# Attention, two feed-forward layers on one core: the first silu placed behind a root, other banks seeded, and copies of Strassen products put first in their step

## Chip, core and metric

The kernel runs on one core of a Trainium2 chip. The metric is the device time of one execution in microseconds (us), median of several runs. It has four compute engines that matter here: TensorE (PE, matmuls), VectorE (DVE), ScalarE (ACT) and GpSimd (POOL); SyncE (SP) issues most DMAs.

## What is computed

Causal attention over 2 x 12 heads (448 positions, 64 wide), then a feed-forward layer with a hard-swish-like gate, then a second one with RMS norm and silu(gate) * value. Cut to the parts that matter:

```python
x = attention(q, k, v)                      # 896 tokens x 768
h = x @ w_in                                # 768 -> 2048
x = (h * clip(h + 3, 0, 6) / 6) @ w_out     # 2048 -> 768
xn = x / sqrt(mean(x * x) + 1e-6) * rms_g   # the root, per token
g = xn @ w_gate                             # 768 -> 1536
val = xn @ w_val
return (g / (1 + exp(-g)) * val) @ w_out2   # 1536 -> 768
```

The weights arrive as float64 and are turned into float32 on the chip. Every product is made of three passes (`mm3`, L205 to L214): each operand is split into a high part and a low part (names that end in hi and lo), and hi*hi, hi*lo and lo*hi are added in one PSUM bank.

## The kernel before

The 896 tokens stand in two groups of 448 (g = 0 and 1), and a matmul is 128 x 128 by 448 columns. Work is recorded in steps: a loop (L974 to L985) runs, in each step, first what is due (`begin_step`), then takes matmuls from the generator `products`, nine to a step once attention is over (`AFTER`). `at(delay, fn)` puts a function at the end of the list of a later step, `soon(fn)` puts it at the front of the next step's list. So the steps set the order of the instructions on each engine, and nothing else does: an engine takes them in that order, and waits where an operand isn't there.

`ff1_out` makes the second layer's input y, and `ff1_y`, `rms_sum` and `rms_root` make the RMS factor of a group. For a group: a matmul with ones (n, L604) sums the squares over partitions, ACT takes the root (L608), DVE the reciprocal (L609), DVE scales the six tiles of y (L621), and `y_split` and `y_low` split them (ACT L627, DVE L634). For group 1 this falls into the time in which PE already works on group 0 of `ff2_plain`.

`ff2_plain` makes the first two (`PLAIN`) column tiles of gate and value for both groups, by plain products: eight products of 18 matmuls, in PSUM banks f0_0 to f0_3 (group 0: gate, value, gate, value) and f1_0 to f1_3 (group 1). `ff2_gate` takes the silu of a gate bank (ACT L695), `ff2_val` multiplies it by the value bank (DVE L700). Two value banks are then kept in the list `spare`:

```python
            if n == 0:
                at(1, ff2_gate, g, m, ps)
            else:
                at(2, ff2_val, g, m, ps)
                if m == PLAIN - 1:
                    spare.append(ps)
```

Here m is 1 for f0_3 and f1_3, so these two are kept.

`ff2_strassen` makes the other ten column tiles m = 2 to 11, both groups at once, as seven products a tile (Strassen-Winograd, q = 1 to 7; below "product (q,m)"), nine matmuls each. For m = 2 and 3 they are interleaved in the order (1,2) (1,3) (2,2) (2,3) (7,2) (6,2) (7,3) (5,2) (6,3) (4,2) (5,3) (3,2) (4,3); from there on a tile is (1,m) (3,m-1) (7,m) (6,m) (2,m) (5,m) (4,m). The products accumulate in three banks: (1,m) and (2,m) in fx_m, (7,m) and (4,m) in fr_m, and (6,m), (5,m), (3,m) in a bank y taken from `spare`, which starts from a copy of (1,m). After each product `ff2_combine` (L856) does one thing: after q = 1 ACT copies fx into y (L861); after 7 ACT copies fr to c22 (L864); after 6 ACT copies y to c21 (L867); after 2 ACT takes the silu of fx (L870); after 5 and 4 DVE adds to c22 and c21 (L873, L876); after 3 DVE multiplies (L882) and gives the bank back to `spare`. So (2,m) must wait until the copy of (1,m) has read fx, and (5,m) until the copy to c21 has read y.

Beside this, weights of the next tiles are made ready by `pair_begin`'s schedule: ACT narrows float64 (L160, L164), DVE joins (L169), subtracts (L777, L798), and both split (ACT L766, L783; DVE L771, L788). The last stage, `strassen`, multiplies by w_out2.

Of the kernel before, what the change touches and what calls it, by code (L numbers as in the profile page):

```python
# [33 lines left out]
PLAIN = 2  # L34
# [17 lines left out]
def fused_kernel(ctx: ExitStack, tc, qa, qb, ka, kb, v, w_in, w_out, w_gate, w_val, w_out2, rms_g, out):  # L52
# [13 lines left out]
    def psum(name):  # L66
        return pspool.tile([128, 512], F32, tag="ps", name=name)
# [21 lines left out]
    def at(delay, fn, *args):  # L89
        due[clock["now"] + delay].append((fn, args))  # L90

    def soon(fn, *args):
        due[clock["now"] + 1].insert(0, (fn, args))
# [103 lines left out]
    def w_tile(n, j):  # L197

        if n not in used and not IN2 <= n < OUT2:
            used.add(n)  # L200
            splits.pop(n - 2, None)
            at(1, w_split)
        return tuple(t[:, j * 128:(j + 1) * 128] for t in splits[n])

    def mm3(ps, w, x, first, last, again=False):  # L205

        whi, wlo = w
        xhi, xlo = x
        nc.tensor.matmul(ps, whi, xhi, start=first, stop=False, skip_group_check=again)  # L209
        yield  # L210
        nc.tensor.matmul(ps, whi, xlo, start=False, stop=False, skip_group_check=again)  # L211
        yield
        nc.tensor.matmul(ps, wlo, xhi, start=False, stop=last, skip_group_check=again)  # L213
        yield  # L214
# [446 lines left out]
    def ff2_plain(w0):  # L661

        for t, (g, i) in enumerate((g, i) for g in range(2) for i in range(4)):
            m, n = divmod(i, 2)
            if t == 0:
                splits.pop(w0 - 2, None)
                splits.pop(w0 - 1)
                at(1, pair_high, PLAIN, 0)
                at(2, pair_low, PLAIN, 0)
                at(4, pair_load, PLAIN + 1, 0)  # L670
                at(5, pair_load, PLAIN + 1, 1)
            elif t == 4:
                pair_begin(PLAIN + 1)
            elif t in (5, 6, 7):
                splits.pop(w0 + t - 5)
            if t == 6:
                at(1, pair_high, PLAIN, 1)
                at(2, pair_low, PLAIN, 1)
            ps = psum(f"f{g}_{i}")[:, :NT]
            for k in range(NK):  # L680
                q = ((1, 2), (0, 4))[g][k // KH]
                yield from mm3(ps, w_tile(w0 + i, k), ops[q, k % KH], k == 0, k == NK - 1)
            if n == 0:
                at(1, ff2_gate, g, m, ps)
            else:
                at(2, ff2_val, g, m, ps)
                if m == PLAIN - 1:
                    spare.append(ps)
        splits.pop(w0 + 3)
        for j in range(KH):  # L690
            ops.pop((0, j))
# [42 lines left out]
    def pair_begin(m):  # L734
        at(1, pair_narrow, m, 0)
        at(2, pair_narrow, m, 1)
        at(3, pair_high, m, 0)
        at(4, pair_low, m, 0)
        at(4, pair_first, m)
        at(5, pair_second, m)  # L740
        at(6, pair_third, m)
        at(7, pair_high, m, 1)
        at(8, pair_low, m, 1)
        if m + 1 < NF2:
            at(4, pair_load, m + 1, 0)
            at(5, pair_load, m + 1, 1)
# [65 lines left out]
    def pair_tile(q, m, j):  # L812
        if q in (5, 6, 7):
            key, o = (m, "t", q), 0
        else:
            key, o = {1: ((m, 0), 0), 2: ((m, 0), 384), 4: ((m, 1), 0), 3: ((m, 1), 384)}[q]
        w = tuple(t[:, o + j * 128:o + j * 128 + 128] for t in ph[key])
        if j == KH - 1 and q not in (1, 4):
            ph.pop(key)
        return w  # L820
# [3 lines left out]
    def ff2_strassen():  # L824
        a, b = PLAIN, PLAIN + 1
        order = [(1, a), (1, b), (2, a), (2, b), (7, a), (6, a), (7, b), (5, a), (6, b), (4, a), (5, b), (3, a), (4, b)]
        for m in range(b + 1, NF2):
            order += [(1, m), (3, m - 1)] + [(q, m) for q in (7, 6, 2, 5, 4)]
        order.append((3, NF2 - 1))
        for q, m in order:  # L830
            if (q, m) == (6, a) or q == 1 and b < m < NF2 - 1:
                pair_begin(m + 2 if m == a else m + 1)
            if q == 1 and m + 1 == NF2:
                state["limit"] = len(srcs)
                for n in range(NC_BUF):
                    at(1 + n, w_load)
                for n in range(NW - 1):
                    at(4 + n + 3 * (n // 3), w_split)
                for p in range(NF2 // 2):
                    at(1 + p // 2, a_fetch, ORDER[0], p)  # L840
                    at(4 + p // 2, a_split, ORDER[0], p)
                for p in range(3):
                    at(5 + p, a_fetch, ORDER[1], p)
            name = {1: "x", 2: "x", 7: "r", 4: "r"}.get(q, "y")
            if q in (1, 7):
                fb[name, m] = psum(f"f{name}_{m}")[:, :NT]
            ps = fb[name, m]
            for j in range(KH):
                yield from mm3(ps, pair_tile(q, m, j), ops[q, j], q in (1, 7) and j == 0, j == KH - 1,
                               q not in (1, 7))  # L850
                if m == NF2 - 1:
                    ops.pop((q, j))
            at(1, ff2_combine, q, m)
        spare.clear()

    def ff2_combine(q, m):  # L856
# [56 lines left out]
    def products():  # L913
        yield from ff1_in(0, 0)
        plan_preps(0, *PREPS[0])
        yield from ff1_in(1, NP1)
        yield from ff1_out(0, 2 * NP1)
        at(1, w_split)
        plan_preps(PREPS[0][2], *PREPS[1])
        pair_early(PLAIN)  # L920
        yield from ff1_out(1, 3 * NP1)
        yield from ff2_plain(IN2)
        yield from ff2_strassen()
        yield from strassen(OUT2)
# [117 lines left out]
```

## Time and profile before

| | |
|---|---|
| median of 3 runs | 576.29 us (575.6 to 584.03) |
| the profiled execution | 577.63 us |
| its span, first to last instruction | 575.8 us |
| busy: PE, DVE, ACT, POOL | 563.0, 411.0, 392.3, 85.3 us |
| granted TensorE clock, mean of the span | 0.994 |

All times of instructions are from the one profiled execution and count from its first instruction. Rows of the timeline give start, duration, engine, source line, operation, output<-inputs, and, in square brackets, how long the engine sat idle just before and what ended that idle time. Names are without buffer numbers: f is any of the banks f0_0 to f1_3, yhi and ylo any split tile of y. Matmuls overlap, so the distance between two starts says more than the duration of one.

### The profile page before, as it was taken

Reading aid. Unit: us, or ns where it says so; the run is one execution under the profiler, and the core shown is the slowest. Engines: PE = TensorE matmul, PEld = TensorE weight load, DVE = VectorE, ACT = ScalarE, POOL = GpSimd, SP = SyncE. Lnnn points to the kernel's source line nnn. Section 1 sums busy time; section 2 is a strip of 40 time slices with the busy share of each in tenths; the row PEclk is TensorE's granted clock in tenths of the full one; section 3 lists DMA queues with packets and bytes.
Section 4 is the critical chain, followed back from the end, with each engine's and each line's share of the span. In section 5 each row is a group of like instructions: output and inputs, shape, how many; then the busy total and the mean of one; then the engine's idle time right before and its main releaser. Section 6 shows DMA issues by size and latency. Waiting matters only on the chain.

```text
span 575.8 us, 9080 instructions
## 1 busy us (share of the span) xinstructions
PE 563.0 (98%) x3048; PEld 491.7 (85%) x3048; DVE 411.0 (71%) x796; ACT 392.3 (68%) x768; POOL 85.3 (15%) x130
## 2 busy tenths in 40 slices
PE   8899999999999999999999999899999999999997
PEld 6567777777899999999999998789999999999996
DVE  4676676767468857555598769969797877866861
ACT  6997878787567768876686778475766565654430
POOL 4665636262100000001001100000000000000000
PEclk9989999999999999999999999999999999999999
DMA  7949776754357888996799913027744517576841
GB/s 217 295 142 280 223 244 204 247 177 142 106 201 254 314 318 295 335 319 225 274 334 387 364 59 141 24 103 271 249 156 181 201 48 258 183 261 205 278 145 64
DMA packets 51231, 125.59 MB, mean 218 GB/s; under 512 B 6768, under 2 KB 30256, under 8 KB 51184
## 3 DMA queue, kind: packets, MB, share of 16 engines
q1 hardware_dynamic: 50752, 124.66, 63.2%
q8 instruction: 24, 0.39, 0.3%
q10 hardware_dynamic: 432, 0.34, 0.2%
q14 instruction: 23, 0.19, 0.1%
HBM read 93.36 MB, written 31.62 MB: 217 GB/s over the span
## 4 chain that ended last, share of the span: by engine, by line
PE 79%; ACT 8%; DVE 7%; DMA 3%; issue 2%; SPq 0%; POOL 0%; ACTq 0%; DVEq 0%
PE h L213 7%; PE h L209 7%; PE h L211 7%; PE y L209 5%; PE y L213 5%; PE y L211 5%; PE o L396 4%; PE t L370 4%; PE s L319 4%; PE f L211 3%; PE f L213 3%; PE f L209 3%; ACT sm L336 3%; PE fr L213 2%; PE fr L211 2%; PE fr L209 2%
## 5 line engine op out<-in xcount | busy, mean ns | idle before, releaser
L185 ACT CAST whi<-c 128x768 fp32r<-128x768 f32 x89 | 74.1, 835 | 40.2 <-DVE c L169 18.0
L191 DVE TENSOR_TENSOR wlo<-c,whi 128x768 fp32r<-128x768 f32 x89 | 88.2, 994 | 18.3 <-ACT whi L185 16.7
L213 PE MATMUL h<-xh,wlo 128*128 128x448 f32 x192 | 72.0, 375 | 0.0
L211 PE MATMUL h<-xl,whi 128*128 128x448 f32 x192 | 70.9, 369 | 0.0
L209 PE MATMUL y<-ghi,whi 128*128 128x448 f32 x192 | 70.5, 367 | 0.0
L209 PE MATMUL h<-xh,whi 128*128 128x448 f32 x192 | 70.4, 367 | 0.0
L213 PE MATMUL y<-ghi,wlo 128*128 128x448 f32 x192 | 70.0, 365 | 0.0
L211 PE MATMUL y<-glo,whi 128*128 128x448 f32 x192 | 69.3, 361 | 0.0
L354 POOL TENSOR_SCALAR sm<-sm,st 112x112 f32<-112x112 f32 (+1 forms) x96 | 55.7, 598 | 69.1 <-ACT pt L380 30.7
L336 ACT ACTIVATE sm<-sm,st 112x112 f32<-112x112 f32 (+3 forms) x96 | 49.5, 522 | 4.2 <-DVE st L329 4.2
L169 DVE SCALAR_TENSOR_TENSOR c<-c,raw 128x768 uint32<-128x768 uint32 x36 | 36.6, 1015 | 18.3 <-ACT raw L164 12.5
L213 PEld LDWEIGHTS h<-xh,wlo 128*128 128x128 f32 x192 | 36.0, 188 | 9.3 <-issue 6.7
L329 DVE CUSTOM_DVE_ANT_0 sm<-s,mask 112x112 f32<-112x112 f32 (+3 forms) x96 | 37.2, 443 | 9.2 <-PE s L319 9.0
L433 DVE SCALAR_TENSOR_TENSOR t<-t,h 128x448 f32<-128x448 f32 x32 | 19.7, 617 | 27.1 <-ACT t L429 27.0
L213 PEld LDWEIGHTS y<-ghi,wlo 128*128 128x128 f32 x192 | 35.9, 187 | 3.7 <-issue 0.2
L211 PEld LDWEIGHTS h<-xl,whi 128*128 128x128 f32 x192 | 36.0, 188 | 2.7
L211 PEld LDWEIGHTS y<-glo,whi 128*128 128x128 f32 x192 | 36.0, 188 | 2.7
L209 PEld LDWEIGHTS h<-xh,whi 128*128 128x128 f32 x192 | 36.2, 188 | 2.5
L209 PEld LDWEIGHTS y<-ghi,whi 128*128 128x128 f32 x192 | 36.0, 188 | 2.5 <-issue 0.2
L429 ACT ACTIVATE t<-h,half 128x448 f32<-128x448 f32 x32 | 20.3, 635 | 25.4 <-PE h L213 25.4
L370 PE MATMUL t<-ident,sm 112*112 112x112 f32 x240 | 33.6, 272 | 2.8 <-POOL sm L354 2.4
L600 POOL TENSOR_TENSOR sq<-sq,sq 128x448 f32<-128x448 f32 x8 | 9.9, 1238 | 171.4 <-ACT sq L589 164.0
(174 smaller groups left out, 1353.1 us busy)
## 6 DMA issues: line engine op xcount, KB each, us to landing
raw<-in_w_in SPq DMA_DIRECT2D x16, 768.0 KB, 5.4
raw<-in_w_out SPq DMA_DIRECT2D x16, 768.0 KB, 6.6
braw<-in_w_out SPq DMA_DIRECT2D x12, 768.0 KB, 6.3
c<-kept SPq DMA_DIRECT2D x21, 384.0 KB, 3.2
a<-left SPq DMA_DIRECT2D x35, 224.0 KB, 3.6
praw<-in_w_gate SPq DMA_DIRECT2D x10, 768.0 KB, 4.5
praw<-in_w_val SPq DMA_DIRECT2D x10, 768.0 KB, 6.4
keptin<-c SPq DMA_DIRECT2D x16, 384.0 KB, 2.7
```

The lines of the kernel that those rows point to most:

```text
L169: nc.vector.scalar_tensor_tensor(bits, bits, 3, z, ALU.logical_shift_left, ALU.bitwise_or)
L185: nc.scalar.copy(hi, c)
L191: nc.vector.tensor_sub(lo, c, f32(hi))
L209: nc.tensor.matmul(ps, whi, xhi, start=first, stop=False, skip_group_check=again)
L211: nc.tensor.matmul(ps, whi, xlo, start=False, stop=False, skip_group_check=again)
L213: nc.tensor.matmul(ps, wlo, xhi, start=False, stop=last, skip_group_check=again)
L319: nc.tensor.matmul(ps[:C, o:o + n], tq[64 * j:64 * j + 64, i * C:(i + 1) * C], tk[64 * j:64 * j + 64, 0:n], start=True, stop=True)
L329: nc.vector.tensor_tensor_reduce(dst, src, mask[:, S - n:], scale=-0.125, scalar=3e38, op0=ALU.add, op1=ALU.min, accum_out=st[u][:, 0, c:c ...
L336: nc.scalar.activation(dst, dst, AF.Exp, scale=-1.0, bias=st[u][:, 0, c:c + 1], accum_out=st[u][:, 1, c:c + 1])
L354: nc.gpsimd.tensor_scalar(t[:, o:o + n], t[:, o:o + n], c, 1.0, op0=ALU.mult, op1=ALU.mult)
L370: nc.tensor.transpose(banks[-1][:C, o:o + C], t[:, o0 + kc * C:o0 + (kc + 1) * C], ident[:C, :C])
L396: nc.tensor.matmul(ps[64 * j:64 * j + 64, HS - n:HS], tv[:, kc, 64 * j:64 * j + 64], t[:, o:o + n], start=kc == 0, stop=kc == nk - 1)
```

## The change

Three places. The silu of the very first gate bank is put three steps after its product instead of one. The two banks kept for the Strassen products are the value banks of group 0 (f0_1, f0_3) instead of the second value bank of each group (f0_3, f1_3). And `ff2_combine` is put at the front of the next step's list instead of its end.

```diff
             if n == 0:
-                at(1, ff2_gate, g, m, ps)
+                at(1 if t else 3, ff2_gate, g, m, ps)
             else:
                 at(2, ff2_val, g, m, ps)
-                if m == PLAIN - 1:
+                if g == 0:
                     spare.append(ps)
...
-            at(1, ff2_combine, q, m)
+            soon(ff2_combine, q, m)
```

On ACT, where group 1's root is taken (sq1_0 gets the root, n1 is the bank of summed squares, t0_0 and t0_1 are the silu of gate banks f0_0 and f0_2; - is before, + is now):

```order
 L766 CAST phi2_0_3942<-pe2_0_384_3750 128x384
+L608 ACTIVATE sq1_0_3414<-n1_3968,eps_73 128x448
 L695 ACT_TABLE_LOAD
-L695 ACTIVATE t0_0_3970<-f0_0_3925 128x448
-L608 ACT_TABLE_LOAD
-L608 ACTIVATE sq1_0_3414<-n1_3968,eps_73 128x448
+L695 ACTIVATE t0_0_3995<-f0_0_3925 128x448
 L627 CAST yhi0_0_4011<-y1_0_3412 128x448
 L627 CAST yhi0_1_4014<-y1_1_3513 128x448
 L627 CAST yhi0_2_4029<-y1_2_3652 128x448
 L627 CAST yhi4_0_4032<-y1_3_3744 128x448
-L695 ACT_TABLE_LOAD
```

The root now stands ahead of the first silu, and of the three table loads here one is left, between the root and the silu.

On ACT, at the first two Strassen products (fx_2 and fx_3 hold (1,2) and (1,3)):

```order
-L861 COPY f0_3_4018<-fx_2_4235 128x448
-L861 COPY f1_3_4207<-fx_3_4245 128x448
+L861 COPY f0_1_3959<-fx_2_4235 128x448
+L861 COPY f0_3_4018<-fx_3_4245 128x448
 L870 ACTIVATE s0_2_4275<-fx_2_4235 128x448
```

The two copies stand where they stood, but write other banks: the second one wrote f1_3, and now writes f0_3.

On ACT, a few products later, after (7,2) and (6,2) (c22_2 is the copy after (7,2), c21_2 the one after (6,2); pc4_0 and pc4_1 are the gate and value weights of tile 4):

```order
-L627 CAST yhi3_0_4301<-y0_3_3169 128x448
-L864 COPY c22_2_4304<-fr_2_4278 128x448
+L864 COPY c22_2_4301<-fr_2_4278 128x448
+L627 CAST yhi3_0_4303<-y0_3_3169 128x448
 L160 ACTIVATE pc4_0_4306<-praw4_0_4130 128x768
 L164 ACTIVATE praw4_0_4130<-praw4_0_4130 128x768
-L160 ACTIVATE pc4_1_4320<-praw4_1_4163 128x768
+L867 COPY c21_2_4319<-f0_1_3959 128x448
+L160 ACTIVATE pc4_1_4322<-praw4_1_4163 128x768
 L164 ACTIVATE praw4_1_4163<-praw4_1_4163 128x768
-L867 COPY c21_2_4325<-f0_3_4018 128x448
```

The copy to c22_2 moved ahead of one cast, and the copy to c21_2 ahead of the two narrowing instructions of the value weights.

## Rows read from the trace of the kernel before

**Rows 1.** The page, part 1: busy us (share of the span), instructions, by engine.

```profile
PE 563.0 (98%) x3048; PEld 491.7 (85%) x3048; DVE 411.0 (71%) x796; ACT 392.3 (68%) x768; POOL 85.3 (15%) x130
```

**Rows 2.** PE's waits in the whole span: line, releaser, us, times, longest.

```profile
PE fx L209 <- ACT f L861: 2.6, 1, 2.6
...
PE f L211 <- DVE ylo L634: 1.0, 1, 1.0
...
PE f L209 <- ACT c L867: 0.6, 1, 0.6
```

**Rows 3.** PE's timeline at its three waits and at the matmul n.

```profile
338.66 0.91 PE L604 MATMUL n<-sq,ones 128*128 128x448 f32 x2
...
339.62 0.37 PE L209 MATMUL f<-yhi,whi 128*128 128x448 f32 x1
...
348.71 0.37 PE L209 MATMUL f<-yhi,whi 128*128 128x448 f32 x1
350.09 0.48 PE L211 MATMUL f<-ylo,whi 128*128 128x448 f32 x1 [1.01 <-DVE ylo L634]
...
369.83 0.36 PE L213 MATMUL fx<-yhi,plo 128*128 128x448 f32 x1
372.80 0.47 PE L209 MATMUL fx<-yhi,phi 128*128 128x448 f32 x1 [2.61 <-ACT f L861]
...
379.99 0.37 PE L213 MATMUL fr<-yhi,ptlo 128*128 128x448 f32 x1
380.96 0.47 PE L209 MATMUL f<-yhi,pthi 128*128 128x448 f32 x1 [0.60 <-ACT c L867]
```

**Rows 4.** Stretches: length, busy us (instructions) by engine, granted clock, DMA share, GB/s.

```profile
333.40:364.57 31.17, 30.16 (x147) 27.29 (x146) 26.42 (x41) 24.54 (x40) 0.00 (x0) 1.00 0.20 72
364.57:392.00 27.43, 24.22 (x119) 21.80 (x117) 21.62 (x39) 16.57 (x28) 0.00 (x0) 1.00 0.22 83
392.00:495.79 103.79, 103.79 (x514) 96.26 (x513) 84.73 (x138) 65.01 (x111) 0.00 (x0) 1.00 0.56 197
345.67:373.20 27.53, 23.91 (x117) 21.50 (x116) 27.39 (x49) 18.58 (x33) 0.00 (x0) 1.00 0.21 77
```

**Rows 5.** ACT's timeline around group 1's root.

```profile
338.87 1.28 ACT L695 ACT_TABLE_LOAD   x1
340.16 0.55 ACT L695 ACTIVATE t<-f 128x448 f32<-128x448 f32 x1
340.72 1.28 ACT L608 ACT_TABLE_LOAD   x1
342.02 0.63 ACT L608 ACTIVATE sq<-n,eps 128x448 f32<-128x448 f32 x1
...
348.52 1.28 ACT L695 ACT_TABLE_LOAD   x1
```

**Rows 6.** DVE's timeline: reciprocal, first low parts, the multiplication of f1_3.

```profile
342.69 2.95 DVE L609 RECIPROCAL sq<-sq 128x448 f32<-128x448 f32 x1 [2.32 <-ACT sq L608]
...
349.42 3.30 DVE L634 TENSOR_TENSOR ylo<-y,yhi 128x448 fp32r<-128x448 f32 x6
...
371.53 0.61 DVE L700 TENSOR_TENSOR t<-f,t 128x448 f32<-128x448 f32 x1
```

**Rows 7.** ACT's timeline at the second copy of (1,m) and at c21_2.

```profile
372.23 0.52 ACT L861 COPY f<-fx 128x448 f32<-128x448 f32 x1 [5.12 <-DVE t L700]
...
376.80 0.53 ACT L864 COPY c<-fr 128x448 f32<-128x448 f32 x1 [0.82 <-PE fr L213]
377.23 0.90 ACT L160 ACTIVATE pc<-praw 128x768 f32<-128x768 f32 x1
...
380.40 0.51 ACT L867 COPY c<-f 128x448 f32<-128x448 f32 x1
...
381.55 0.57 ACT L627 CAST yhi<-y 128x448 fp32r<-128x448 f32 x1
```

**Rows 8.** ACT's waits in the whole span: line, releaser, us, times, longest.

```profile
ACT c L864 <- PE fr L213: 19.3, 9, 2.4
```

## Prediction

> **What bounds the kernel now.** I read the page first: PE is busy 98% of the span [rows 1], so time is won only where PE stands still, or by giving it less to do, and the change takes no matmul away. Next I read the list of what PE waits for [rows 2]. Outside attention it has three entries: 2.6 us for the copy L861, 1.0 us for a low part L634, 0.6 us for the copy L867. Each happens once. Then I read PE's timeline at these places [rows 3], because an idle figure leaves out the slow restart, and the stretches around them [rows 4], because they give PE's undisturbed pace. From 392.00 to 495.79 PE runs 57 products of nine matmuls without a wait: 103.79 / 513 = 0.2023 us from start to start [rows 4]. The granted clock is 1.00, the level of 2.4 GHz, in every one of these stretches, so the waits cost their own length and nothing in clock.
>
> With this pace the waits are priced. From 333.40 to 364.57 PE has 144 matmuls: 29.13 us of 31.17. Of the 2.04 us that are left, the matmul n takes 0.76: a start at 338.66, and the next L209, which would have come at 338.86 without n, at 339.62 [rows 3]. So the wait for L634 costs 1.28. From 364.57 to 392.00 there are 13 products, 117 matmuls: 23.67 us of 27.43, so the two copies cost 3.76 together. The restarts split this: 369.83 to 372.80 is 2.97 where 0.20 is normal, 379.99 to 380.96 is 0.97 [rows 3]; with 0.11 each for a slow second start, 2.88 and 0.88. **All that can be won at these places is 1.28 + 2.88 + 0.88 = 5.04 us.**
>
> **First edit: the silu behind the root.** Now ACT loads a table at 338.87, takes the silu, loads another at 340.72 and starts the root at 342.02 [rows 5]; DVE has been idle 2.32 us when the root lets the reciprocal go at 342.69 [rows 6]. The root's operand, the bank of n, is done at 338.66 + 0.91 = 339.57 [rows 3]. With the root first in line and no table load ahead of it, it starts at about 339.6, 2.4 us sooner. Silu and its load follow: 339.6 + 0.63 + 1.28 + 0.55 = 342.1, before DVE, which sits in the reciprocal until 343.2, can want its result, so the delayed silu costs nothing. The third load (1.28 us at 348.52) goes too; it is ACT time that PE does not wait for.
>
> What follows on DVE is one unbroken queue: 27.39 us busy of the 27.53 from 345.67 to 373.20 [rows 4]. It all moves up by 2.4. The low part that PE waits for until 350.09 is then there at 347.7; PE wants it 0.20 after 348.71. That wait goes, with 1.2 us to spare: the term is 1.28. Its ends are 1.28 and 0 (if the root came less than 1.2 us sooner, a part would be left).
>
> **Second edit: other seeded banks.** The second copy L861 sat idle for 5.12 us, ended by DVE's L700, and (2,3) on PE waited for the copy [rows 7, 3]. The reason is f1_3: the copy writes the bank that L700 at 371.53 [rows 6] still has to read, and L700 stands at the end of DVE's long queue. Now the copy writes f0_3, a bank of group 0, whose multiplication stands far ahead of this one in DVE's queue. What is late next is (1,3) itself. PE reaches (1,2) at 364.57 - 1.28 = 363.29, and with 1.82 us a product (1,3) ends at about 367.1; the copy takes 0.52, to 367.7; (2,3) is due at 363.29 + 3 x 1.82 = 368.75. The wait goes with 1 us to spare, and the term is 2.88. Behind it PE takes (7,2) at 370.6. Everything that DVE had queued ahead of L700 is done by 371.53 - 2.4 = 369.1, so no low part is late there. Holding f0_1 instead of f1_3 ties up no additional bank: of eight, five are in use at (7,2) (f0_1, f0_3, fx_2, fx_3, fr_2) and f1_3 until its L700. If that cover failed, PE would wait for f1_3's L700 again, and at most the 2.88 would come back.
>
> **Third edit: copies first.** At (5,2) the copy to c21_2 is late because four narrowing instructions stand before it, 377.23 to 380.40, 3.17 us [rows 7]. Counted from the start of the copy to c22_2 (376.80), PE wants (5,2) 3.39 us later (379.99 + 0.20) and gets it after 4.16. In the new order only two of the four come before it, and the cast L627: 0.43 + 0.57 + 1.59 + 0.51 = 3.10. That is 0.3 us in time, so the term is 0.88; its ends are 0.88 and, if that thin margin fails, about 0. For the later tiles PE has no wait now, so the reorder can win nothing there; what it can lose is the third rival. Stores to DRAM on SP move by one or two places with the sums that feed them; they wait for DVE, and the DMA share is 0.22 and 0.56 in these stretches [rows 4], so they cost nothing.
>
> **Sum.** 5.04 us off the profiled span of 575.8 gives 570.8. The profiled execution lasted 577.63, 1.8 us around its span, so it becomes 572.6. The median of the runs is 1.3 us below that execution, 576.29, and I predict against the median: 571.3 us, 0.9% less. That is within 2%, which is about what a measurement of this kernel can tell from no change.
>
> **The rivals.**
>
> *A part comes back, at (5,2) or at (3,2).* Without its waits, the stretch from (1,2) on takes 23.67 us, and DVE's 21.62 us of work [rows 4] fill it by 91%. The sums of the products now stand ahead of the splits of the operands for q = 3, so one of these may be late for (3,2), or the copy of c21_2 misses its 0.3 us. One wait of the size of the one measured, 0.9, to one of 2.5 (the first two terms without the rest): 572.2 to 573.8. For it: DVE was without a gap for 27 us just before. Against it: that queue gets 2.4 us ahead.
>
> *The change doesn't do what it says.* DVE's queue is the real limit, and PE waits as long, only elsewhere: 576.3. For it: 27.39 of 27.53 us busy. Against it: the costliest wait hangs on a bank, not on what DVE makes, and DVE idles 2.32 us at the root [rows 6], which is exactly what is given back to it.
>
> *Slower: copies at the head of the queue.* For the eight tiles 4 to 11, copies and sums that need a product just finished now stand before casts and splits of the next tile's weights, and hold these up while they wait for PE. The trace shows that such waits exist: the copy L864 sat 19.3 us idle in 9 cases, up to 2.4 each [rows 8]. The Trainium skill, "PSUM — Partial Sum Buffer", section "Engine vs sequencer instructions", says that the queues of ScalarE and VectorE are strictly first in, first out, so nothing overtakes a waiting copy; the trace agrees, in that no ACT instruction runs in the 5.12 us before the copy L861 [rows 7]. By that rule alone every such copy would pass its wait on. In this kernel it costs time if weights are late by more than PE allows: the change then loses from 5.04 / 8 = 0.63 us a tile on. With the wait measured at L867, 0.88 a tile, it is 7.0 - 5.0 = 2.0 us slower: 578.3. Against it: PE needs those weights about a tile later, 63 matmuls or 12.7 us, and in the stretch with these tiles ACT is busy 65.01 and DVE 84.73 of 103.79 us [rows 4], while PE waits for neither.
>
> **Chances.** The forecast 0.72, a part coming back 0.17, no effect 0.06, slower 0.05. The range 569.6 to 575.0 holds the first two with the scatter of the runs, some 1 to 2 us (575.6 and 576.29 unprofiled, 577.63 profiled), and leaves out the last two. No case comes near 2% (564.8 or 587.8): faster by over 2% 0.02, within 2% 0.96, slower by over 2% 0.02.
>
> **What would show it.** Right: one table load between root and silu; the reciprocal at about 340.3; none of the three entries in the list of PE's waits; the stretch from the first product of `ff2_plain` to (1,4) about 53.6 us instead of 58.6; a span near 570.8. Wrong: PE waiting for L867 at (5,2) or for L634 at (3,2) (the first rival); DVE without a gap and PE waiting for several of its low parts (the second); PE waiting for L788, L783 or L771 between (1,4) and the last stage (the third).

## The result, and the profile after

The change takes 572.6 us (median of 6 runs, 571.68 to 572.75) against 577.24 (6 runs, 575.6 to 584.03). The means stand as 0.9899 to 1, 95% interval 0.985 to 0.9948; the medians as 0.992, because the one run at 584.03 weighs on the mean. That is about one per cent faster, within 2%, and inside the predicted range; the predicted time was 571.3. The profiled execution has a span of 571.0 us, lasted 572.75, and does what the prediction said row by row.

The page, part 1, answers to [rows 1]: ACT has two instructions fewer, PE as many.

```profile
PE 562.2 (98%) x3048; PEld 491.8 (86%) x3048; DVE 410.4 (72%) x796; ACT 390.6 (68%) x766; POOL 85.5 (15%) x130
```

The list of PE's waits, whole, answers to [rows 2]: the three entries L861, L634 and L867 are gone. What is left belongs to attention and to the start.

```profile
PE t L370 <- POOL sm L354: 2.3, 3, 1.4
PE warm L933 <- DVE ones L927: 1.0, 1, 1.0
PE o L396 <- ACT pt L380: 1.0, 1, 1.0
PE o L396 <- DMA v<-in_v: 0.4, 1, 0.4
PE s L319 <- ACT pt L380: 0.2, 1, 0.2
```

The stretches (length, busy us and instructions by engine, granted clock, DMA share, GB/s) answer to [rows 4]. The first is from the first product of `ff2_plain` to (1,2), the second from there to (1,4), the third from there to the last stage. PE's busy time equals the length in all three.

```profile
333.58:363.46 29.88, 29.88 (x148) 27.37 (x146) 27.26 (x43) 22.50 (x40) 0.00 (x0) 1.00 0.19 69
363.46:387.14 23.68, 23.68 (x118) 21.95 (x117) 18.80 (x35) 13.97 (x24) 0.00 (x0) 1.00 0.25 89
387.14:490.94 103.80, 103.80 (x515) 96.25 (x513) 85.38 (x140) 66.03 (x111) 0.00 (x0) 1.00 0.54 193
```

Below, "stage" is the sum of the first two: 29.88 + 23.68 = 53.56 us, where before had 58.60. The difference is 5.04 us, the sum of the prediction to the digit, against the one execution of before from which the prediction took its prices.

ACT around the root answers to [rows 5]:

```profile
339.80 0.64 ACT L608 ACTIVATE sq<-n,eps 128x448 f32<-128x448 f32 x1 [1.79 <-PE n L604]
340.45 1.28 ACT L695 ACT_TABLE_LOAD   x1
341.74 0.55 ACT L695 ACTIVATE t<-f 128x448 f32<-128x448 f32 x1
```

The bracket is the point: ACT now waits for PE's n (1.79 us), and PE no longer waits, later, for what hangs on ACT's root. DVE, against [rows 6], has the reciprocal, the first low parts and the multiplication of f1_3 2.2 us sooner, or 2.4 us counted from PE's first product of `ff2_plain`, which came 0.18 us later in this execution:

```profile
340.47 2.95 DVE L609 RECIPROCAL sq<-sq 128x448 f32<-128x448 f32 x1 [0.95 <-ACT sq L608]
...
347.20 3.29 DVE L634 TENSOR_TENSOR ylo<-y,yhi 128x448 fp32r<-128x448 f32 x6
...
369.31 0.61 DVE L700 TENSOR_TENSOR t<-f,t 128x448 f32<-128x448 f32 x1
```

The first of these low parts is there at about 347.8, and PE takes it at 349.11:

```profile
349.11 0.36 PE L211 MATMUL f<-ylo,whi 128*128 128x448 f32 x1
```

ACT's copies, against [rows 7]: both copies of (1,m) now wait for PE's product, none for DVE, and the copy to c21_2 starts at 375.24.

```profile
365.48 0.52 ACT L861 COPY f<-fx 128x448 f32<-128x448 f32 x1 [1.80 <-PE fx L213]
367.30 0.52 ACT L861 COPY f<-fx 128x448 f32<-128x448 f32 x1 [1.30 <-PE fx L213]
...
372.76 0.53 ACT L864 COPY c<-fr 128x448 f32<-128x448 f32 x1 [1.22 <-PE fr L213]
373.19 0.57 ACT L627 CAST yhi<-y 128x448 fp32r<-128x448 f32 x1
...
375.24 0.53 ACT L867 COPY c<-f 128x448 f32<-128x448 f32 x1
```

That copy ends at 375.77, and PE begins (5,2) at 376.21, as soon as its pace allows:

```profile
376.01 0.37 PE L213 MATMUL fr<-yhi,ptlo 128*128 128x448 f32 x1
376.21 0.36 PE L209 MATMUL f<-yhi,pthi 128*128 128x448 f32 x1
```

The margin is 0.44 us, where the prediction had 0.3.

### The profile page after: what moved, and what is told of

Read it like the earlier page. It is cut to its first block, busy times and chain, and to the rows that moved or that the text cites. A ratio compares the mean times of both kernels' runs of the same rounds, so it can differ in the third digit from the quotient of the medians.

```text
span 571.0 us, 9072 instructions
## 1 busy us (share of the span) xinstructions
PE 562.2 (98%) x3048; PEld 491.8 (86%) x3048; DVE 410.4 (72%) x796; ACT 390.6 (68%) x766; POOL 85.5 (15%) x130
## 4 chain that ended last, share of the span: by engine, by line
PE 95%; ACT 3%; DMA 1%; SPq 0%; issue 0%; DVE 0%
PE y L209 8%; PE y L213 8%; PE y L211 8%; PE h L213 7%; PE h L209 7%; PE h L211 7%; PE f L209 5%; PE f L213 5%; PE f L211 5%; PE s L319 4%; PE o L396 4%; PE t L370 4%; PE fx L209 2%; PE fr L213 2%; PE fx L213 2%; PE fr L211 2%
```

## The experiments

All but the last ran once each, with a profile (the kernel before and the third edit alone again, below); they are read from the stage, not from the time of the run, because the stage shows a few tenths that the time hides. The undisturbed values are 29.87 us up to (1,2) and 23.68 from there to (1,4).

**The first edit alone.**

```diff
-                at(1, ff2_gate, g, m, ps)
+                at(1 if t else 3, ff2_gate, g, m, ps)
```

> Only the first edit (silu behind the root). Stage = from the first product of ff2_plain to (1,4), 58.60 us before and 53.56 with the whole change. Theory A (the three waits hang together through DVE's queue): the wait for L634 goes (1.28), and since DVE's queue moves up by 2.2 while PE moves up by 1.28, the multiplication of f1_3 frees the bank sooner against PE, so the wait for the copy L861 shrinks by about 1.0 too: stage 56.3, waits left in the list L861 1.6 and L867 0.6. Theory B (the terms are independent): only 1.28 goes, stage 57.3, L861 stays 2.6.

The stage took 29.87 + 26.33 = 56.20 us, span 573.5. From PE's list, the two entries of the three that are left:

```profile
PE fx L209 <- ACT f L861: 1.5, 1, 1.5
...
PE f L209 <- ACT c L867: 0.6, 1, 0.6
```

The copy's wait costs 26.33 - 23.68 - 0.87 = 1.8 with its restart instead of 2.88, though nothing was done to the copy. Theory A holds: counted from PE's first product of `ff2_plain`, the L700 of f1_3 came 2.4 us sooner (after 35.73 us, at 369.21, instead of 38.13) while PE came 1.3 us sooner, and the wait shrank by the difference, 1.1. Against the first trace of before the first edit alone is worth 2.4 us, and not 1.28: 1.1 off the second wait, and the whole first wait, which was long in that trace (see below).

**The second edit alone, and another bank.**

```diff
-                if m == PLAIN - 1:
+                if g == 0:
                     spare.append(ps)
```

> Only the second edit (banks of group 0 are seeded). Theory A (PE waits for the reader of f1_3, nothing else): the wait for L861 goes, stage 58.60 - 2.88 = 55.7, waits left L634 1.0 and L867 0.6. Rival (DVE's queue is the limit): PE then waits for low parts (L634, L788) at (7,2) or (6,2) instead, stage about 58.

Stage 30.31 + 24.55 = 54.86, span 572.3. The wait for L861 is gone; L867 is left with 0.6, and L634 is there with only 0.2, of which more below. No low part is late behind (7,2), so DVE's queue is not what PE waited for.

```diff
-                if m == PLAIN - 1:
+                if (g, m) in ((0, 1), (1, 0)):
                     spare.append(ps)
```

> The kernel before with one other bank: the second seeded bank is f1_1 (first value bank of group 1) instead of f1_3. Theory A (what counts is when DVE's L700 has read the bank: f1_1's L700 ended at about 366.7, before the copy wants the bank at 368.5): the wait for L861 goes as in the run with the second edit alone, stage 55.7. Rival (a bank of group 1 is late in any case): stage 58.6 and L861 still at 2.6.

Stage 30.88 + 24.55 = 55.43, span 572.7, no entry for L861. So it is not group 1 that is late: f1_1, a bank of group 1 that DVE has read two products sooner, does as well as a bank of group 0.

```profile
PE f L211 <- DVE ylo L634: 0.7, 1, 0.7
PE f L209 <- ACT c L867: 0.6, 1, 0.6
```

**The third edit alone.**

```diff
-            at(1, ff2_combine, q, m)
+            soon(ff2_combine, q, m)
```

> Only the third edit (copies and sums first in their step). Theory A: only the wait for L867 at (5,2) goes, 0.88: stage 57.7, waits left L634 1.0 and L861 2.6, no new one in tiles 4 to 11. Rival (copies at the head of the queue hold up the weights): new waits for L783, L788 or L771 in tiles 4 to 11, 0.63 us a tile or more, and the span is longer than before (575.8).

L867 is gone from the list and there is no new wait in tiles 4 to 11 (103.80 us, as before). But the stage took 30.86 + 28.12 = 58.98, not 57.7. The second stretch should have lost 0.88 of 27.43. The stretches show where the rest went: behind the wait for L861 the granted clock is 0.54 for 3.7 us.

```profile
368.00:372.80 4.80, 2.19 (x11) 1.71 (x10) 4.17 (x8) 0.98 (x2) 0.00 (x0) 1.00 0.28 66
372.80:376.50 3.70, 3.70 (x13) 3.27 (x12) 0.00 (x0) 0.54 (x1) 0.00 (x0) 0.54 0.88 340
376.50:391.64 15.14, 15.14 (x76) 14.04 (x75) 11.26 (x20) 11.63 (x19) 0.00 (x0) 1.00 0.09 36
```

In this stretch some 9 matmuls stood 0.37 us apart instead of 0.20. Above 23.68 and the wait's 2.88, the second stretch is 1.56 us too long. That called for repeats, further down.

**The change without one of its edits.** These start from the changed kernel and put one line back. First the silu:

```diff
-                at(1 if t else 3, ff2_gate, g, m, ps)
+                at(1, ff2_gate, g, m, ps)
```

> The change without its first edit. Theory A: the wait for L634 is back, 1.28: stage 54.8 (58.60 before, 53.56 with the whole change), one entry left, L634 1.0. If the late root also made operands late behind (7,2), the stage would be 55.5 or more.

Stage 30.78 + 23.68 = 54.46, one entry, L634 with 0.6: 0.91 us with its restart. Then the banks:

```diff
-                if g == 0:
+                if m == PLAIN - 1:
                     spare.append(ps)
```

> The change without its second edit (f0_3 and f1_3 are seeded as before). Theory A: with the root early the wait for the copy into f1_3 is back at about 1.9 with its restart, not 2.88: stage 55.5, L861 1.6 in the list. Independent terms: stage 56.4, L861 2.6.

Stage 29.87 + 25.46 = 55.33, one entry, L861 with 1.5: 1.78 with its restart, the same as with the first edit alone. The terms are not independent. Last the place in the step:

```diff
-            soon(ff2_combine, q, m)
+            at(1, ff2_combine, q, m)
```

> The change without its third edit (combine stays at the end of the step's list). Theory A: the wait for L867 at (5,2) is back, 0.88: stage 54.4, L867 0.6 in the list, tiles 4 to 11 the same. If the reorder costs anything in tiles 4 to 11, the stretch from (1,4) to the last stage is shorter here than with the whole change (103.8).

Stage 29.87 + 24.54 = 54.41, one entry, L867 with 0.6: 0.86. The tiles from (1,4) on took 103.79 us, with the change 103.80: putting copies first costs nothing there, and wins nothing.

**One step further.** The copies and sums run at once, and not first in the next step:

```diff
-            soon(ff2_combine, q, m)
+            ff2_combine(q, m)
```

> More of the suspected cost: ff2_combine is issued in the step of its product, one step (1.82 us of PE) earlier still, so that ACT and DVE stand longer at the head of their queues. With the change the low parts of a tile are ready 6.1 to 6.7 us before PE wants them, 7.7 before the change. Theory A: the extra hold-up is about 1.8 us and eats 2 of the 6 us, no wait in tiles 4 to 11, stretch (1,4) to the last stage 103.8, span 570.5 to 571.5. Rival (head of the queue): weights are late, waits for L788, L783 or L771 in the list, span 575 or more.

The stage is unchanged (29.87 + 23.69), and no weight is late, but tiles 4 to 11 took 104.91 us instead of 103.80, span 572.0, between the two forecasts. The missing 1.1 us stand at (6,4) and (6,5):

```profile
392.26 0.37 PE L213 MATMUL fr<-yhi,ptlo 128*128 128x448 f32 x1
393.22 0.47 PE L209 MATMUL f<-yhi,pthi 128*128 128x448 f32 x1 [0.60 <-ACT f L861]
```

ACT's timeline has the reason: the silu L887, now one step sooner too, sat 6.03 us at the head of ACT's queue for DVE's sum, with two narrowing instructions and then the copy L861 behind it.

```profile
390.58 0.58 ACT L887 ACTIVATE c<-c 128x448 f32<-128x448 f32 x1 [6.03 <-DVE c L876]
391.06 0.89 ACT L160 ACTIVATE pc<-praw 128x768 f32<-128x768 f32 x1
391.86 0.88 ACT L164 ACTIVATE praw<-praw 128x768 uint32<-128x768 uint8 x1
392.63 0.54 ACT L861 COPY f<-fx 128x448 f32<-128x448 f32 x1
```

So the third rival's mechanism exists, one step away from where the change put the copies, and it came at a copy that others held up, not at the weights. It was 1.1 us in all, not 0.63 a tile. The weights had less time in hand than the expectation says: with the change the low part of the weights of (7,5) was ready at 399.20 and PE took it at 403.93, 4.7 us later, the shortest such time in these tiles.

**What varies from run to run.**

The kernel before ran twice more, unchanged, and the third edit alone once more.

> The kernel before, unchanged, for two things that the first runs left open. (1) The wait for L634 was 1.0 us in the first trace of before and 0.2 to 0.7 in four other kernels whose root is as late. Theory: ACT's queue comes to the root when the weights from DRAM let it, PE comes to f1_0 in its own time, so the cost of this wait varies from run to run, 0.4 to 1.3 us. Rival: it is a property of the edits, and before shows 1.0 again. (2) With the third edit alone the granted clock was 0.54 from 372.8 to 376.5, just behind the wait for L861, which cost 1.6 us more. Theory: this belongs to the 2.6 us wait, and the kernel before shows it in some executions as well (stage 60.2 instead of 58.6). Rival: it comes from the edit.

> The same once more: L634 anywhere from 0.2 to 1.0; stage from the first product of ff2_plain to (1,4) either 57.8 to 58.6 with the clock at 1.00 throughout, or 59.4 to 60.2 with the clock near 0.5 for some 3 us behind the wait for L861.

> The third edit alone once more. If the low clock behind the wait for L861 came by chance, it can be absent here: stage 57.1 to 57.7 with clock 1.00, L861 2.6. If the edit causes it, it is there again: stage near 59.

The two repeats of the kernel before had stages of 59.02 and 58.94 us, spans 576.4 and 576.3, and the list names L861 with 2.6 and L867 with 0.6 but not L634. Both show the low clock: here the stretches of the first.

```profile
333.54:363.55 30.01, 30.01 (x147) 27.30 (x146) 26.13 (x40) 23.74 (x40) 0.00 (x0) 1.00 0.19 69
363.55:372.30 8.75, 6.13 (x30) 5.36 (x29) 8.65 (x17) 2.83 (x6) 0.00 (x0) 1.00 0.03 12
372.30:375.80 3.50, 3.50 (x11) 3.09 (x10) 0.00 (x0) 0.60 (x2) 0.00 (x0) 0.51 0.99 363
375.80:392.56 16.76, 16.15 (x81) 14.64 (x79) 12.99 (x22) 13.14 (x21) 0.00 (x0) 1.00 0.14 54
```

And its matmuls: 0.20 us from start to start before the wait, 0.37 behind it.

```profile
368.60 0.37 PE L211 MATMUL fx<-ylo,phi 128*128 128x448 f32 x1
368.81 0.36 PE L213 MATMUL fx<-yhi,plo 128*128 128x448 f32 x1
371.79 0.47 PE L209 MATMUL fx<-yhi,phi 128*128 128x448 f32 x1 [2.62 <-ACT f L861]
...
373.78 0.57 PE L209 MATMUL fx<-yhi,phi 128*128 128x448 f32 x1
374.15 0.57 PE L211 MATMUL fx<-ylo,phi 128*128 128x448 f32 x1
```

The third edit alone, repeated, had no low clock: second stretch 26.36, that is 2.68 above the undisturbed value for a wait of 2.4. So the low clock comes with the long wait and not with the edit: three of the five traces with this wait at 2.4 to 2.6 us have it, and none of the nine others, where it was 1.5 or gone: there the clock is 1.00 from the first product of `ff2_plain` to (1,4). It costs 1.6 us.

The wait for L634 varies too, and the traces with the late root say how. Here the start of the table load on ACT is counted from PE's first product of `ff2_plain`, and the cost is the first stretch less 29.87:

```text
run                            table load after   cost of the wait
third edit alone, repeated           3.97              0.00
before, second repeat                4.26              0.09
before, first repeat                 4.32              0.14
second edit alone                    4.60              0.44
change without its first edit        5.08              0.91
third edit alone                     5.16              0.99
other bank                           5.19              1.01
before                               5.47              1.30
```

The cost is what lies above 4.17, to 0.02 us. ACT's queue and PE arrive at this place each in its own time, and the cost is the gap between them. With the first edit there is no such gap: the root waits for n, which PE makes, and the first stretch is 29.87 or 29.88 in all five traces that have the edit (29.33 in a sixth, where n itself was made shorter, below).

**A faster version.** The prediction priced n, the matmul that sums squares, at 0.76 us of PE time. The experiment gives it one pass:

```diff
-            nc.vector.tensor_add(ri[g], ri[g], s)
+            total = slot([128, NT], f"tot{g}", F32R)
+            nc.vector.tensor_add(total, ri[g], s)
...
-        nc.tensor.matmul(ps, ones, ri[g], start=True, stop=True)
+        nc.tensor.matmul(ps, ones_r, total, start=True, stop=True)
```

> The change, and the matmul n (the sum of squares over partitions) with operands in the fp32r format instead of fp32, so that its sum is a little less exact. If n's cost of 0.76 us on PE (in place of 0.20) is real PE time, both groups' n save 0.56 each: span 571.0 - 1.1 = 569.9, time 571.5. If it is hidden, the span stays 571.0. Against the kernel before: ratio 0.988, with 0.990 for the change alone.

571.51 us (4 runs, 570.86 to 571.67), ratio 0.9886 to before (0.9869 to 0.9902), span 569.7. In the trace n is one matmul of 0.37 us, and the stage is 29.33 + 23.69 = 53.02: 0.54 less for group 1. The same was won for group 0: from its n to the first product of `ff2_plain` it is 53.18 us, with the change 53.73. It is the fastest of the kernels here, though by its interval it can't be told from the change alone; the stage tells it. Its sum of squares is less exact.

```profile
L606 PE MATMUL n<-tot,ones_r x2: 366/367/368, 279.7 to 338.1; 128*128 128x448 f32 x2
```

## Why the prediction was right, and what was off

**What bounds the kernel.** PE did, and all that was won was won at its three waits: the stage lost 5.04 us where 5.04 was forecast, and the rest kept its length (103.79 and 103.80 us for tiles 4 to 11, 80.0 behind them). That the sum meets to the digit is in part luck: the stage after has no wait left and repeats, but against the two repeats of before it would be 5.46 and 5.38, by a low clock that was not priced and a first wait that was nearly absent. PE's pace from the undisturbed stretch (0.2023 us) was the tool that got this: the idle figures of [rows 2] add up to 4.2 and would have fallen short by the slow restarts.

**First edit.** Right in mechanism: the root started at 339.80 (forecast 339.6), DVE came 2.4 us sooner against PE (forecast 2.4), the low parts were there 1.3 us before PE wanted them (forecast 1.2), the delayed silu cost nothing. The size, 1.28, was that of one execution: in eight traces with the late root it was 0 to 1.30, 0.61 on average. The bound "0" of this term was named for another reason (a root that gains too little).

**Second edit.** Right: the wait hung on the reader of one bank, as the run with another bank of group 1 shows. The term 2.88 was the wait and its restart, and was mis-sized downward: in three of five traces with this wait, a low clock behind it cost 1.6 us more. The prediction said that "the waits cost their own length and nothing in clock", from a trace in which this was so.

**Third edit.** Right, 0.88 forecast, 0.86 and 0.87 measured; the margin that replaced it is 0.44 us instead of 0.3.

**The sum's base.** The step that put the time 1.3 us low is the last one: the sum against the profiled execution, 577.63 - 5.04 = 572.6, is the measured median, and the prediction then moved it to the lower median of three runs. Of the runs of before, that one was on the quick side: the larger samples have medians of 577.24 and 577.9. The runs of before scatter by some 3.5 us (575.6 to 579.15, one at 584.03 aside), those of the change by 1.1. The traces show three things that vary: the low clock behind the long wait (1.6 us) and the cost of the late root (up to 1.3), both gone with the change, and the start of `ff2_plain`, 332.66 to 335.23 us, which varies whatever the edits. Which of them made a run without a trace longer isn't shown.

**The rivals.** No part came back at (5,2) or (3,2). That the change would do nothing fell with the second edit alone. The slower rival's mechanism was found one step further on, and it cost 1.1 us and not 7: the weights had 4.7 us or more in hand, and what was held up was a copy. The first rival's upper price of 2.5 us does not follow from the terms that it names (the first two add up to 4.16); nothing hung on it, since no part came back.

**Taken one by one, the terms don't add up.** The first edit alone won 2.4 us of 58.60 because it also took 1.1 off the second wait. Alone, the second takes all of that one. Whoever measures edits singly counts that part twice.

## What to carry to other kernels

Price a wait by PE's start-to-start pace over a whole stretch, not by its idle entry, and look at the granted clock just behind it in short stretches, since a slice of the page is too wide to show 3.5 us at half clock. Where two engines reach a meeting point each in its own time, one trace gives one draw of the cost (0 to 1.30 us here, where the first trace had the most); tying the one to the other takes the draw away. A bank that must be reused is best taken from the tile whose reader comes first, and copies that PE waits for go to the front of a step, but not a step further: here that put a silu which waited 6 us ahead of a copy that PE waited for.

## What had not been expected

After a single wait of 2.4 to 2.6 us on a PE that was busy before and after, the granted clock fell to about 0.51 (the 1.2 GHz level) for some 3.5 us in three of five traces and stayed at 1.00 in two. In the first repeat of before it was 1.00 up to 372.30, half a us after PE had started again, and 1.00 again from 375.80. Most traces of either order have a low stretch in attention too, in the first trace of before from 26.4 to 33.2 us; it lies ahead of the stage, and the mean clock of 0.994 of that trace comes from there. What decides between the two cases was not tried. The burst of transfers that follows the wait does not decide it by itself: the DMA share is 0.88 and 0.99 in the stretches at the low clock above, and here is the first trace of before, as busy with the clock at 1.00.

```profile
374.00:378.00 4.00, 4.00 (x22) 3.71 (x21) 0.63 (x1) 2.20 (x4) 0.00 (x0) 1.00 0.92 370
```

The Trainium skill, "TensorE: Matmul & The Clock Gate", section "What's actually happening", says that the gate gives full clock by how busy the engine has lately been, which fits a fall that shows just behind a wait; no run here shows how it decides.
